# The result stage of an attention and gated feed-forward kernel: fifteen block products of 2x3x3 blocks in place of seven of 2x2x2

## The chip, the cores and the metric

The kernel runs on one core of a Trainium2 chip. The metric is device time in microseconds, from one launch to its end. Three runs of the kernel before took 972.55, 970.60 and 970.07 us, a median of 970.6 us. One profiled execution is described here: its own time was 970.28 us, and the span that its trace covers is 967.9 us, so 2.4 us lie outside the trace.

## The reference, cut to what matters

Banded causal attention (8 batches, 8 heads, 576 positions, head size 64, window 128, with a bias per head), and then a gated feed-forward network over its 4608 tokens:

```python
attn_out = _attn_ref(q, k, v)                     # softmax over a window of 128, times v
x = attn_out.transpose(0, 2, 1, 3).reshape(4608, 512)
gate = 1.0 / (1.0 + np.exp(-(x @ w_gate)))        # w_gate, w_val: 512 x 1536
val = x @ w_val
return (gate * val) @ w_out                       # w_out: 1536 x 512
```

All inputs and outputs are float32, and the kernel's matrix products have float32 accuracy: every operand is split into a rounded part ("hi") and the rest ("lo"), and one product of two operands is three matmuls (hi*hi, lo*hi, hi*lo).

## The kernel before, in words

The work is in three stages. In the first (to about 283 us of the span) the attention of 32 units of two heads runs, and beside it the gate and value projections of the first four feature blocks for the first 2560 tokens (`gates1`, matmuls on L583). In the second (`gates2`, matmuls on L668, 283.65 to 706.72 us) the other projections run. In the third (`results`, matmuls on L794, from 704.00 us) the hidden values, which the stages before left in DRAM (`hs`), are multiplied by `w_out`, and the output is written.

The second and third stages don't multiply blocks one by one. `gates2` takes a round of tokens, cuts it in two halves and the features in two, and forms seven products of sums of blocks where a plain 2x2x2 block product has eight (the products are numbered 0 to 6, made in the order 0, 3, 4, 1, 5, 2, 6). The widths of the halves stand in `HALVES`, one number a round: 512, 384, 384, 512, 512. `results` of before does the same with the hidden values: five rounds of the same widths; the feed-forward dimension is cut in two quadrants of 768 and the tokens in two halves. For each of the seven products it goes through three thirds of 256 features (`e`): it forms the sum of quadrants that the product needs (`add`, L762, in place), splits it into hi and lo (`parts`: a cast by `copy` on L233 or L234, a subtraction by `minus` on L243) and makes two groups of six matmuls (`six`), one for each half `i` of a 256-wide output block. A product ends in two PSUM banks. `keep` (ScalarE, L805) and `total` (VectorE, L810) take the sums out of the banks, and `store` writes them to the output.

The sums of weight blocks are made once, in `combine`: `keepw` first decodes `w_out` (it comes as 64-bit words), writes it to DRAM (`wod`), and `combine` reads it back, makes four sums of 256 columns and splits seven blocks into hi and lo, six times. The tiles `wos` then stay in SBUF for all five rounds.

The order of the work is not written by hand. Each step is added to a graph (`g.add`) with its engine, a cost, what it reads and writes and a wish for its time; `rank` and `order` then lay all steps on the engines' queues by these costs. A step may have several ways: a cast goes to ScalarE or VectorE, a sum that reads no PSUM to VectorE or GpSimd. Each engine works its queue strictly in that order, SyncE (which issues all DMAs) too. The tiles that hold hi and lo of a product (`cxA` with three places, `cxB` with three, `cxC` with one) are used in rotation, so a cast waits until the matmuls that read its place are done.

Of the kernel before, what the change touches and what calls it, by code (L numbers as in the profile page):

```python
# [28 lines left out]
HALVES = (512, 384, 384, 512, 512)  # L29
# [3 lines left out]
HC = NFC // 6  # L33
NRING, NRING1, NHC = 6, 4, 7
# [25 lines left out]
SEEDS = ()  # L60

# [148 lines left out]

@with_exitstack
def attention_gated_ffn(ctx: ExitStack, tc: tile.TileContext, qd, kd, vd, wg, wv, wo, out):
# [24 lines left out]
    def move(out, src, reads, writes, want, kb):  # L237
        g.add("SP", 0.6, lambda: nc.sync.dma_start(out(), src()), reads, writes, want, size=kb / 330.0,
              store=writes[0][0] in ("hs", "xs", "wod", "out"))
# [40 lines left out]
    hs = [[dram.tile([NFC // 2, P, HALVES[b // 2]], F32, name=f"hs{k}_{b}") for b in range(2 * NT2)] for k in range(2)]  # L280
    wod = [dram.tile([P, DM], F32, name=f"wod{f}") for f in range(NFC)]
# [29 lines left out]
    hr = lambda: T(moe, "hr", [P, 2, NFC // 2, N2], F32, tag="wA")  # L311
    hw = lambda: T(moe, "hw", [P, NFC // 2, N2], F32, tag="xW")
# [3 lines left out]
    wot = lambda c, part_: T(name=f"wos{c}", **wtag((c + 4) % 6))[:, part_]  # L316
# [6 lines left out]
    def decode(src, bits, kb, keys, want):  # L323
# [3 lines left out]
        if src.dtype == F32:  # L327
# [3 lines left out]
        g.add("ACT", act_cost(DM), lambda: nc.scalar.mul(as32(bits()), as32(wraw(s)[:, :, 1]), 2.0 ** -112), [kr, *keys], [kb], want)  # L331
        g.add("DVE", dve_cost(DM), lambda: nc.vector.tensor_scalar(
            bits(), bits(), 3, None, op0=ALU.logical_shift_left), [], [kb], want, port=True)
        for word, scalar, o0 in ((0, 29, ALU.logical_shift_right), (1, -0x80000000, ALU.bitwise_and)):
            g.add("DVE", dve_cost(DM, two=True), lambda word=word, scalar=scalar, o0=o0: nc.vector.scalar_tensor_tensor(  # L335
                bits(), wraw(s)[:, :, word], scalar, bits(), op0=o0, op1=ALU.bitwise_or), [kr], [kb], want, port=True)

    def parts(hi, lo, val, n, reads, k0, k1, want):
        copy(hi, val, n, reads, [k0], want)
        minus(lo, val, lambda: as32(hi()), n, [*reads, k0], [k1], want)  # L340
# [398 lines left out]
    hq0 = lambda: T(moe, "hq0", [P, NFC // 2, N2], F32, tag="xr")  # L739
    hquad = lambda h, k: hr()[:, k] if h else hw() if k else hq0()  # L740

    def hcombo(s, part_):
        return combo(ORDER[s], part_)

    def results(t):
        F, N, t0 = FIRST + 2, HALVES[t], EDGE[2 * t]
        third = [slice(e * HC, (e + 1) * HC) for e in range(3)]
        hk = {(h, k, e): [("hq", h, k, e)] for h in range(2) for k in range(2) for e in range(3)}
        for h, k in ((0, 0), (1, 0), (1, 1), (0, 1)):
            for e in range(3):  # L750
                move(lambda h=h, k=k, e=e: hquad(h, k)[:, third[e], 0:N], lambda h=h, k=k, e=e: hs[k][2 * t + h][third[e]].rearrange("c p t -> p c t"),
                     [("hs", k, 2 * t + h, c) for c in range(e * HC, (e + 1) * HC)], hk[h, k, e], F, HC * P * N / 256)
        slots = {(k, e): (3 * n + e) % NHC for n, k in enumerate(ORDER) for e in range(3)}
        m = HC * N

        def split(k, e, val, reads):
            s = slots[k, e]
            parts(lambda: hcombo(s, 0)[:, :, 0:N], lambda: hcombo(s, 1)[:, :, 0:N], val, m, reads, ("hc", s, 0), ("hc", s, 1), F)

        def add(o, a, b, op, reads, writes):  # L760
            way = ("POOL", 0.1 + m * 0.00223, True, lambda: nc.gpsimd.tensor_tensor(o(), a(), b(), op=op))
            g.add("DVE", dve_cost(m, two=True), lambda: nc.vector.tensor_tensor(o(), a(), b(), op=op), reads, writes, F,  # L762
                  port=True, ways=[way])

        bx, bz, by = [], [], []
        some = {}
        bk = lambda b: (lambda: mm[b][:, 0:N])

        halved = lambda k, i: t == NT2 - 1 and k == 6 and i == 1

        def product(k, banks_, start):
            for e in range(3):
                v = lambda a, b, e=e: (lambda: hquad(a, b)[:, third[e], 0:N])
                q = lambda a, b: hk[a, b, e]
                if k == 3:
                    add(v(1, 0), v(1, 0), v(1, 1), ALU.add, q(1, 1), q(1, 0))
                elif k == 4:
                    add(v(1, 0), v(1, 0), v(0, 0), ALU.subtract, q(0, 0), q(1, 0))
                elif k == 5:
                    add(v(0, 1), v(0, 1), v(1, 0), ALU.subtract, q(1, 0), q(0, 1))  # L780
                    add(v(1, 0), v(1, 1), v(1, 0), ALU.subtract, q(1, 1), q(1, 0))
                a, b = {0: (0, 0), 3: (1, 0), 4: (1, 0), 1: (0, 1), 5: (1, 0), 2: (0, 1), 6: (1, 1)}[k]
                split(k, e, v(a, b), q(a, b))
                s = slots[k, e]
                for i in range(2):
                    if len(banks_) == i:
                        banks_.append(bank())

                    last = halved(k, i) and e == 2
                    for a, b in ((0, N // 2), (N // 2, N)) if last else ((0, N),):  # L790
                        def six(i=i, e=e, s=s, a=a, b=b):
                            for c in range(HC):
                                for j, (xp, wp) in enumerate(((0, 0), (0, 1), (1, 0))):
                                    nc.tensor.matmul(mm[banks_[i]][:, a:b], wot(e * HC + c, wp)[:, k, i * P:(i + 1) * P], hcombo(s, xp)[:, c, a:b],  # L794
                                                     start=(start and e == c == j == 0), stop=(e == 2 and c == HC - 1 and j == 2),
                                                     skip_group_check=True)
                        wa = 0 if k < 1 else 1
                        g.add("PE", 3 * HC * ((b - a) / 2400 + 0.0133), six,
                              [("hc", s, 0), ("hc", s, 1)] + [("wo", e * HC + c, p, wa) for c in range(HC) for p in range(2)] + [("mm", banks_[i])] * (a > 0),
                              [("mm", banks_[i], 1) if a else ("mm", banks_[i])], 1.0e6)  # L800

        def keep(name, banks_, i, a=0, e=N):
            s = some[name, i] = some[name, i] if a else scratch()
            b = banks_[i]
            g.add("ACT", act_cost(e - a, psum=True), lambda: nc.scalar.mul(ring2(s)[:, a:e], mm[b][:, a:e], 0.5),  # L805
                  [("mm", b, 1) if a else ("mm", b)], [("rg", s, a) if a else ("rg", s)], F)

        def total(name, banks_, i):
            s, b = some[name, i], banks_[i]
            g.add("DVE", dve_cost(N, psum=True), lambda: nc.vector.scalar_tensor_tensor(  # L810
                ring2(s)[:, 0:N], bk(b)(), 0.5, ring2(s)[:, 0:N], op0=ALU.mult, op1=ALU.add), [("mm", b)], [("rg", s)], F)

        def store(name, i, h, d, a=0, e=N):
            s = some[name, i]
            r = (d * 2 + i) * P
            c0 = t0 + h * N
            move(lambda: out[r:r + P, c0 + a:c0 + e], lambda: ring2(s)[:, a:e], [("rg", s, a) if a else ("rg", s)], [("out", r, c0 + a)], F, (e - a) / 2)

        two = range(2)
        product(0, bx, True)  # L820
        for i in two:
            keep("a1", bx, i)
        product(3, bz, True)
        for i in two:
            keep("p5", bz, i)
        product(4, bx, False)
        for i in two:
            keep("u2", bx, i)
        product(1, by, True)
        for i in two:  # L830
            total("a1", by, i)
            store("a1", i, 0, 0)
        product(5, bx, False)
        for i in two:
            total("p5", bx, i)
            store("p5", i, 1, 1)
        product(2, bz, False)
        for i in two:
            total("u2", bz, i)
            store("u2", i, 0, 1)  # L840
# [126 lines left out]
    for t in range(NT2):  # L967
        results(t)
# [54 lines left out]
```

## Time and profile before

| | |
|---|---|
| median of three runs | 970.6 us (970.07 to 972.55) |
| the profiled execution's own time | 970.28 us |
| its span | 967.9 us |
| TensorE busy (PE) | 959.4 us, 99% of the span |
| VectorE busy (DVE) | 803.7 us, 83% |
| ScalarE busy (ACT) | 502.4 us, 52% |
| GpSimd busy (POOL) | 175.3 us, 18% |
| result stage on TensorE | 704.00 to 964.23 us |

PE are matmuls, PEld the weight loads, which run beside them. A matmul's record reaches from its start to the end of its way through the array and overlaps the next ones, so what a row of matmuls costs is read from the distance between starts, not from the mean duration. The same holds, to a smaller degree, for VectorE's records. The chain of waits names, for each stretch of time, the work that the end of the program waited for.

### The profile page before, as it was taken

The numbers are of one execution on the slowest core, as the hardware profiler recorded it, in microseconds if no ns is written. First come the engines' busy times: TensorE is split into PE (matmuls) and PEld (weight loads), VectorE is DVE, ScalarE is ACT, GpSimd is POOL, SyncE is SP. The second block draws the span as 40 slices with busy tenths as digits, with TensorE's granted clock in tenths as the row PEclk, the third lists the DMA queues.
The fourth block names the chain that finished last, engine by engine and source line by source line (L and its number), as shares of the span: only waits on it lengthen the run. The fifth ranks groups of instructions, "written<-read, shape, count | busy, mean of one in ns | idle before, by whom it ended". The sixth has DMA issues, their size and how long they took to land.

```text
span 967.9 us, 18446 instructions
## 1 busy us (share of the span) xinstructions
PE 959.4 (99%) x6562; PEld 818.0 (85%) x6562; DVE 803.7 (83%) x1807; ACT 502.4 (52%) x1268; POOL 175.3 (18%) x333
## 2 busy tenths in 40 slices
PE   9999999999999999999999999999999999999998
PEld 7777877877788889999988888888888999988887
DVE  7998888999699975475979948897999889898882
ACT  6998978797645543344634434553563233332320
POOL 6555656666301100000000100000000000000000
PEclk9999999999999999999999999999999999999999
DMA  8877767875365313145566512548346263637101
GB/s 305 270 263 267 245 233 256 281 250 189 118 210 175 120 55 128 58 136 169 169 193 204 186 65 75 162 148 280 108 147 190 93 180 101 227 99 238 44 22 65
DMA packets 83610, 162.67 MB, mean 168 GB/s; under 512 B 9408, under 2 KB 35008, under 8 KB 83520
## 3 DMA queue, kind: packets, MB, share of 16 engines
q1 hardware_dynamic: 83520, 161.51, 50.6%
q8 instruction: 51, 0.84, 0.4%
q14 instruction: 39, 0.32, 0.1%
HBM read 111.15 MB, written 50.33 MB: 167 GB/s over the span
## 4 chain that ended last, share of the span: by engine, by line
PE 92%; DVE 4%; ACT 2%; issue 1%; POOL 1%; ACTq 0%; POOLq 0%; DVEq 0%
PE mm L668 44%; PE mm L794 27%; PE mm L583 10%; PE mm L416 5%; PE mm L464 3%; PE mm L525 3%; ACT pb L435 1%; DVE pb L432 1%; PE mm L501 1%; DVE mm L424 1%; DVE pb L458 1%; POOL pt L475 1%; DVE work L335 0%; PE mm L298 0%; DVE x L243 0%
## 5 line engine op out<-in xcount | busy, mean ns | idle before, releaser
L668 PE MATMUL mm<-cxA,w2s 128*128 128x512 f32 (+1 forms) x684 | 161.5, 372 | 0.0
L668 PE MATMUL mm<-cxB,w2s 128*128 128x512 f32 (+1 forms) x684 | 161.4, 372 | 0.0
L233 ACT COPY ring<-mm 128x512 f32<-128x512 f32 (+1 forms) x142 | 78.3, 552 | 130.3 <-PE mm L668 109.3
L668 PEld LDWEIGHTS mm<-cxA,w2s 128*128 128x128 f32 x684 | 125.8, 188 | 18.3
L668 PEld LDWEIGHTS mm<-cxB,w2s 128*128 128x128 f32 x684 | 125.8, 188 | 18.2
L583 PE MATMUL mm<-x,w 128*128 128x512 f32 x480 | 135.0, 411 | 0.0
L435 ACT ACTIVATE pb<-pb,st 128x128 f32<-128x128 f32 x288 | 113.1, 397 | 19.7 <-DVE st L432 18.9
L475 POOL TENSOR_SCALAR_AFFINE_SELECT pt<-both 128x384 f32<-128x384 f32 x192 | 106.5, 579 | 70.5 <-ACT both L233 57.1
L794 PE MATMUL mm<-cxA,wos 128*128 128x512 f32 (+1 forms) x540 | 113.5, 367 | 0.0
L794 PE MATMUL mm<-cxB,wos 128*128 128x512 f32 (+1 forms) x540 | 113.3, 367 | 0.0
L794 PEld LDWEIGHTS mm<-cxA,wos 128*128 128x128 f32 x540 | 98.4, 188 | 12.7
L794 PEld LDWEIGHTS mm<-cxB,wos 128*128 128x128 f32 x540 | 98.4, 188 | 12.6
L583 PEld LDWEIGHTS mm<-x,w 128*128 128x128 f32 x480 | 84.9, 189 | 17.7 <-issue 3.1
L242 POOL TENSOR_TENSOR work<-work 128x256 f32<-128x256 f32 x23 | 20.9, 910 | 420.3 <-DVE work L335 221.3
L679 ACT ACTIVATE sg<-mm 128x512 f32<-128x512 f32 (+1 forms) x96 | 54.1, 564 | 72.9 <-DVE mm L675 42.5
L675 DVE TENSOR_TENSOR mm<-mm,ring 128x512 f32<-128x512 f32 (+1 forms) x96 | 62.2, 649 | 27.4 <-PE mm L668 27.3
L335 DVE SCALAR_TENSOR_TENSOR work<-work 128x512 int32<-128x512 int32 x104 | 69.7, 688 | 0.8
L416 PE MATMUL mm<-kr,qr 64*64 64x192 f32 (+2 forms) x1280 | 67.6, 322 | 1.5 <-DVE st L432 1.3
L432 DVE CUSTOM_DVE_ANT_0 pb<-mm,relm 128x128 f32<-128x128 f32 x288 | 68.6, 278 | 0.0
L424 DVE COPY_PREDICATED mm<-swap,mm 128x256 f32<-128x256 int32 x144 | 55.2, 420 | 12.0 <-PE mm L416 11.9
L416 PEld LDWEIGHTS mm<-kr,qr 64*64 64x64 f32 x1280 | 43.5, 133 | 22.7 <-issue 12.2
L805 ACT ACTIVATE ring<-mm 128x512 f32<-128x512 f32 (+2 forms) x41 | 22.3, 547 | 72.1 <-PE mm L794 72.1
(111 smaller groups left out, 1554.1 us busy)
## 6 DMA issues: line engine op xcount, KB each, us to landing
hs<-ring SPq DMA_DIRECT2D x72, 256.0 KB, 2.4
kr<-in_k_dram SPq DMA_DIRECT2D x31, 576.0 KB, 5.2
work<-in_moe_w_gate_dram SPq DMA_DIRECT2D x20, 512.0 KB, 4.2
work<-in_moe_w_val_dram SPq DMA_DIRECT2D x20, 512.0 KB, 4.5
qr<-in_q_dram SPq DMA_DIRECT2D x31, 320.0 KB, 5.9
vr<-in_v_dram SPq DMA_DIRECT2D x32, 288.0 KB, 4.2
xs<-xt SPq DMA_DIRECT2D x32, 288.0 KB, 4.0
hr<-hs SPq DMA_DIRECT2D x18, 512.0 KB, 4.5
```

What stands on the lines that cost most here:

```text
L233: g.add("ACT", act_cost(n, psum), lambda: nc.scalar.copy(out(), src()), reads, writes, want, release=release, ways=[("DVE", dve_cost(n, ps ...
L335: g.add("DVE", dve_cost(DM, two=True), lambda word=word, scalar=scalar, o0=o0: nc.vector.scalar_tensor_tensor(bits(), wraw(s)[:, :, word], ...
L416: nc.tensor.matmul(sp[j // 2][col, j % 2, c0:c0 + n], qraw(u)[row, i // 2, col], kraw(u)[row, k1:k1 + n], start=True, stop=True)
L424: g.add("DVE", dve_cost(4 * D, psum=True), lambda b=b: nc.vector.copy_predicated(fold[b][:, :, 1:3], swaps, fold[b][:, :, 3::-3]), [], [(" ...
L432: g.add("DVE", 0.21, lambda: nc.vector.tensor_tensor_reduce(pb()[:, e], sp[j // 2][:, j % 2, D:D + P], relm[u.p][:, w], op0=ALU.add, op1=A ...
L435: g.add("ACT", 0.39, lambda: nc.scalar.activation(pb()[:, e], pb()[:, e], AF.Exp, bias=st()[:, e:e + 1], scale=-1.0, accum_out=st()[:, 3 + ...
L475: nc.gpsimd.affine_select(pt(u)[:, f0:f0 + 2 * n - 1:2, :], both(), [[0, n], step], cmp, 0.0, base=0, channel_multiplier=mult)
L583: nc.tensor.matmul(mm[s][:, 0:n], w1(kind, wi)[:, i, c * P:(c + 1) * P], x1(x)[:, c, 0:n], start=(k == 0 and c == 0), stop=(k == 2 and c = ...
L668: nc.tensor.matmul(mm[b][:, 0:N], w2t(i, wp)[:, wk, c * P:(c + 1) * P], combo(k, xp)[:, c, 0:N], start=(start and c == 0 and j == 0), stop ...
L675: g.add("DVE", dve_cost(N, psum=True), lambda: nc.vector.tensor_tensor(o(), bk(b)(), a(), op=ALU.add), [("mm", b), *reads] if okeys else r ...
L679: g.add("ACT", act_cost(N, psum=True), lambda: nc.scalar.activation(sg[h](), bk(b)(), AF.Tanh, scale=0.5), [("mm", b)], [("sg", h)], F)
L794: nc.tensor.matmul(mm[banks_[i]][:, a:b], wot(e * HC + c, wp)[:, k, i * P:(i + 1) * P], hcombo(s, xp)[:, c, a:b], start=(start and e == c ...
```

## The change

The result stage becomes a product of 2 by 3 blocks of `w_out` (256 output columns by 512 features) with 3 by 3 blocks of hidden values (512 features by 512 tokens). A plain product of these blocks has 18 block products; the change makes it with 15 products of sums of blocks. A round is now 1536 tokens, and there are three rounds. Each product runs over 512 features in two halves `h`, and for each half there are a split into hi and lo and two groups of six matmuls, all 512 columns wide. The table `RESULTS` says what is added to what: `wadd` and `wform` make the 15 weight blocks, `x` makes the 15 sums of hidden blocks (13 additions a round, in place, in nine groups of buffers) and says where each product stands between them, `out` says into which PSUM banks (`b`) a product goes, which of them it adds to, and which sums of banks and SBUF buffers (`s`) give the six output blocks (`o`). In a round `out` has 11 sums, each for two halves of a block; 10 of the 11 read a PSUM bank.

`nodes` replaces `keepw` and makes the weight sums from the decoded `w_out`, four times (11 sums of 256 columns and 15 stores to DRAM, `w3d`). `loadw` reads a product's weights back in the first round and splits them (a multiplication on ScalarE and one instruction on VectorE); nine of the 15 stay in SBUF, and six (`STREAM`) are written to DRAM as hi and lo (`w3s`) and read again in each later round, `RECENT` = 3 products ahead. The hi and lo of a half product have five places (`combos`) that go round. Hidden values lie in DRAM in blocks of 512 tokens now, and the second and third round of `gates2` are 256 and 512 wide in place of 384 and 384. All the other code is unchanged but for names.

```diff
-HALVES = (512, 384, 384, 512, 512)
+HALVES = (512, 256, 512, 512, 512)
-HC = NFC // 6
-NRING, NRING1, NHC = 6, 4, 7
+NRING, NRING1 = 6, 4
+NP = 15
+RECENT = 3
+STREAM = (2, 4, 7, 9, 12, 14)
+ROUNDS = (0, 1, 2)
+RESULTS = dict(
+    wadd="6=1-0 7=3-4 8=0+3 9=2+8 10=0+2 11=1+3 12=5+9 14=1+4 13=5+14 15=4+5 16=2+13",
...
-    hs = [[dram.tile([NFC // 2, P, HALVES[b // 2]], F32, name=f"hs{k}_{b}") for b in range(2 * NT2)] for k in range(2)]
-    wod = [dram.tile([P, DM], F32, name=f"wod{f}") for f in range(NFC)]
+    hs = [[dram.tile([KC, P, NB], F32, name=f"hs{k}_{t}") for t in range(NT // NB)] for k in range(3)]
+    w3d = [dram.tile([P, KC, 2 * P], F32, name=f"wd{p}") for p in range(NP)]
+    w3s = [dram.tile([P, KC, 4 * P], F32, name=f"ws{p}") for p in range(NP)]
...
+    def nodes(j):
...
+        for token in RESULTS["wadd"].split():
+            d, x, op, y = term(token)
+            d, x, y = (raw3(int(v)) if int(v) < 6 else int(v) for v in (d, x, y))
+            sums(lambda d=d: piece(d), lambda x=x: piece(x), op, lambda y=y: piece(y), 2 * P, pk(x) + pk(y), pk(d), W)
...
+    combos, banked, rest = Pool((54, 58, 62, 42, 46)), Pool(range(8)), Pool((*range(103, 109), 109, 110, 94))
...
+    def loadw(p, r):
...
+            if r:
+                move(lambda a=a, n=n: at(a, n).rearrange("p (j f) -> p j f", j=n), lambda i=i, n=n: w3s[p][:, i:i + n],
+                     [("w3s", p, j) for j in range(i, i + n)], K(a, n), F, 256 * n)
+                continue
+            move(lambda blk=blk: as32(blk(1)), lambda i=i, n=n: w3d[p][:, i:i + n], [("w3d", p, j) for j in range(i, i + n)], K(a, n), F, 128 * n)
+            m, scale = n * 2 * P, 0.5 if RESULTS["wform"].split()[p][0] == "+" else -0.5
+            g.add("ACT", act_cost(m), lambda blk=blk: nc.scalar.mul(blk(0), as32(blk(1)), scale), [], K(a, n), F)
+            g.add("DVE", dve_cost(m, two=True), lambda blk=blk: nc.vector.scalar_tensor_tensor(
+                blk(1), as32(blk(1)), scale, as32(blk(0)), op0=ALU.mult, op1=ALU.subtract), [], K(a, n), F, port=True)
...
+            for h in range(2):
+                spot = lambda r_: groups[r_] + 2 * h
+                for d, x, op, y in adds:
+                    d, x, y = (spot(int(v)) for v in (d, x, y))
+                    sums(lambda d=d: at(d, 2), lambda x=x: at(x, 2), op, lambda y=y: at(y, 2), 2 * NB, K(x, 2) + K(y, 2), K(d, 2), F)
+                c, o = combos.take(), spot(r)
+                split(c, o)
                 for i in range(2):
+                    def six(h=h, c=c, i=i, b=banks_[i]):
+                        for j in range(2):
+                            for k, (xp, wp) in enumerate(((0, 0), (0, 1), (1, 0))):
...
+                    g.add("PE", 6 * (NB / 2400 + 0.0133), six, K(c, 4) + K(w[2 * h]) + K(w[2 * h + 1]), [("mm", banks_[i])], 1.0e6)
+                combos.give(c)
```

VectorE's queue where the gates end and the result stage begins. Before, a row names the line, the operation, the tile written and the tiles read (`mm` are PSUM banks, `hr`, `hq` and `hw` the hidden values, `cxA` to `cxC` the split sums, `wos` the weights, `ring` and `sg` outputs and gates); it lies near the end of the last gate block:

```order
L243 TENSOR_TENSOR cxA<-hq_6707,cxA 128x1024
L243 TENSOR_TENSOR wos_7059<-work,wos_7059 128x256
L243 TENSOR_TENSOR work<-work 128x256
L243 TENSOR_TENSOR wos_7059<-work,wos_7059 128x1536
L675 TENSOR_TENSOR ring<-mm_145,ring 128x512
L243 TENSOR_TENSOR cxB<-hr,cxB 128x1024 x3
L243 TENSOR_TENSOR wos_7104<-work,wos_7104 128x256
L762 TENSOR_TENSOR hr<-hr,hq_6707 128x1024
L243 TENSOR_TENSOR wos_7104<-work,wos_7104 128x1536
L243 TENSOR_TENSOR cxC<-hr,cxC 128x1024
```

In the changed kernel the same place holds the additions (line 801, `xr`, `work` and `ha` are now the nine groups), the splits (line 277), the gate stage's own sums (lines 712 and 720) and a weight split (line 861); its last row is the sixth split of the first round:

```order
L801 TENSOR_TENSOR xr<-work,xr 128x1024
L720 SCALAR_TENSOR_TENSOR ring<-sg_784,mm_169 128x512
L861 SCALAR_TENSOR_TENSOR w2s_6630<-w2s_6630 128x3x256
L720 SCALAR_TENSOR_TENSOR ring<-sg_985,ring 128x512
L277 TENSOR_TENSOR cxA<-work,cxA 128x1024
L712 TENSOR_TENSOR ring<-mm_170,ring 128x512
L277 TENSOR_TENSOR cxB<-work,cxB 128x1024
L801 TENSOR_TENSOR work<-xr,work 128x1024 x2
L801 TENSOR_TENSOR xr<-xr,ha 128x1024
L277 TENSOR_TENSOR cxB<-work,cxB 128x1024
L801 TENSOR_TENSOR xr<-xr,ha 128x1024
L277 TENSOR_TENSOR cxA<-work,cxA 128x1024
```

The weight sums and splits that make `wos` have left this place; in front of the early products there are more additions than before, and the splits of the 15 weight blocks are spread over the whole first round.

VectorE's queue at the start of a later round. Before (the last round but one), an addition and a split take turns:

```order
L762 TENSOR_TENSOR hr<-hr 128x1024
L243 TENSOR_TENSOR cxA<-hq_6707,cxA 128x1024 x2
L762 TENSOR_TENSOR hr<-hr 128x1024
L243 TENSOR_TENSOR cxA<-hq_6707,cxA 128x1024
L762 TENSOR_TENSOR hr<-hr 128x1024
L243 TENSOR_TENSOR cxB<-hr,cxB 128x1024
L810 SCALAR_TENSOR_TENSOR ring<-mm_146,ring 128x384
L762 TENSOR_TENSOR hr<-hr,hq_6707 128x1024
L243 TENSOR_TENSOR cxB<-hr,cxB 128x1024 x2
```

In the changed kernel the second round begins so (from its fourth split to its eighth):

```order
L277 TENSOR_TENSOR cxB<-work,cxB 128x1024
L801 TENSOR_TENSOR work<-xr,work 128x1024
L801 TENSOR_TENSOR xr<-work,xr 128x1024
L801 TENSOR_TENSOR xr<-xr,ha 128x1024
L277 TENSOR_TENSOR cxB<-work,cxB 128x1024
L801 TENSOR_TENSOR work<-xr,work 128x1024
L801 TENSOR_TENSOR work<-work,xr 128x1024
L801 TENSOR_TENSOR xr<-xr,ha 128x1024
L277 TENSOR_TENSOR cxA<-work,cxA 128x1024 x2
L801 TENSOR_TENSOR work<-work,xr 128x1024
L801 TENSOR_TENSOR ha<-ha,xr 128x1024 x2
L277 TENSOR_TENSOR cxA<-work,cxA 128x1024
```

Nine additions stand between five splits here, where before there were four between six.

## Rows read from the trace of the kernel before

**Rows 1.** The page's busy times: engine, us, share of the span, instructions.

```profile
PE 959.4 (99%) x6562; PEld 818.0 (85%) x6562; DVE 803.7 (83%) x1807; ACT 502.4 (52%) x1268; POOL 175.3 (18%) x333
```

**Rows 2.** Chain of waits, in order of time: start us, us, what.

```profile
298.64 405.36 PE mm L668 x1944
704.00 1.36 PE mm L794 x6
...
706.72 257.51 PE mm L794 x1260
```

**Rows 3.** Busy time by stretch: the five result rounds (the second row holds two).

```profile
core 0: us, PE busy (x) PEld busy (x) DVE busy (x) ACT busy (x) POOL busy (x), PEclk, DMA share, GB/s
706.70:763.40 56.70, 56.70 (x254) 47.13 (x253) 53.37 (x59) 22.26 (x27) 0.00 (x0) 1.00 0.54 172
763.40:850.60 87.20, 87.20 (x503) 87.06 (x502) 76.05 (x92) 30.00 (x42) 0.00 (x0) 1.00 0.49 152
850.60:907.60 57.00, 57.00 (x253) 47.18 (x252) 50.42 (x50) 18.00 (x22) 0.00 (x0) 1.00 0.46 150
907.60:964.40 56.80, 56.62 (x256) 46.96 (x254) 35.14 (x37) 10.50 (x15) 0.00 (x0) 1.00 0.09 35
```

**Rows 4.** Timeline of TensorE: start us, us, what; 384 wide, then 512 wide.

```profile
399.62 1.20 PE L668 MATMUL mm<-cxB,w2s 128*128 128x384 f32 x6
400.66 1.20 PE L668 MATMUL mm<-cxA,w 128*128 128x384 f32 x6
...
944.95 8.32 PE L794 MATMUL mm<-cxA,wos 128*128 128x512 f32 x36
953.11 8.32 PE L794 MATMUL mm<-cxB,wos 128*128 128x512 f32 x36
```

**Rows 5.** Timeline of the end, all engines; the 18 are 6 of 512 and 12 of 256 columns.

```profile
961.04 2.97 PEld L794 LDWEIGHTS mm<-cxC,wos 128*128 128x128 f32 x18
961.27 2.95 PE L794 MATMUL mm<-cxC,wos 128*128 128x512 f32 x18
...
964.26 0.66 ACT L805 ACTIVATE ring<-mm 128x256 f32<-128x256 f32 x2 [0.83 <-PE mm L794]
```

**Rows 6.** Groups by shape, 704 to 968 us: busy us, mean ns, idle before, releaser.

```profile
L794 PEld LDWEIGHTS mm<-cxB,wos 128*128 128x128 f32 x540 | 98.4, 188 | 12.6
...
L233 ACT CAST cxB<-hr 128x1024 fp32r<-128x1024 f32 x13 | 13.7, 1053 | 27.7 <-PE mm L794 24.4 <-DVE hr L762 3.3
...
L810 DVE SCALAR_TENSOR_TENSOR ring<-mm,ring 128x512 f32<-128x512 f32 x18 | 12.3, 687 | 8.4 <-PE mm L794 8.4
...
L794 PE MATMUL mm<-cxC,wos 128*128 128x256 f32 x12 | 1.6, 282 | 0.0
```

**Rows 7.** Timeline of VectorE in stretches where it did not wait.

```profile
701.64 0.41 DVE L243 TENSOR_TENSOR wos<-work,wos 128x256 fp32r<-128x256 f32 x1
701.98 0.42 DVE L243 TENSOR_TENSOR work<-work 128x256 f32<-128x256 f32 x1
702.31 1.75 DVE L243 TENSOR_TENSOR wos<-work,wos 128x1536 fp32r<-128x1536 f32 x1
...
889.74 0.68 DVE L810 SCALAR_TENSOR_TENSOR ring<-mm,ring 128x512 f32<-128x512 f32 x1
890.34 1.22 DVE L762 TENSOR_TENSOR hr<-hr 128x1024 f32<-128x1024 f32 x1
891.48 0.68 DVE L810 SCALAR_TENSOR_TENSOR ring<-mm,ring 128x512 f32<-128x512 f32 x1
892.08 1.22 DVE L243 TENSOR_TENSOR cxA<-hq,cxA 128x1024 fp32r<-128x1024 f32 x1
893.21 1.22 DVE L762 TENSOR_TENSOR hr<-hr 128x1024 f32<-128x1024 f32 x1
```

**Rows 8.** Busy time by stretch (columns as in rows 3): two with much DMA.

```profile
0.00:24.20 24.20, 22.40 (x254) 18.48 (x255) 18.36 (x96) 15.81 (x61) 16.07 (x33) 1.00 0.85 305
...
653.40:677.60 24.20, 24.20 (x109) 20.04 (x108) 18.76 (x29) 8.74 (x15) 1.75 (x2) 1.00 0.83 280
```

More of the change, by code (lines that the diff above doesn't have):

```diff
@@ L208, in act_cost, with term, __init__, take @@
     return (0.05 if psum else 0.1) + n * 0.00084
+def term(token):
+    dst, val = token.split("=")
+    op = next(c for c in val if c in "+-_")
+    a, b = val.split(op)
+    return dst, a, op, b
+class Pool:
+    def __init__(self, free):
+        self.free = list(free)
+        self.low = len(self.free)
+    def take(self):
+        x = self.free.pop(0)
+        self.low = min(self.low, len(self.free))
+        return x
+    def give(self, x):
+        self.free.append(x)
 @with_exitstack
@@ L737, in mix @@
         yield 6
[L739 to L784, printed above, removed]
-                for i in range(2):
[L786 to L840, printed above, removed]
-        product(6, bx, False)
-        for i in two:
-            for a, b in ((0, N // 2), (N // 2, N)) if halved(6, i) else ((0, N),):
-                keep("x", bx, i, a, b)
-                store("x", i, 1, 0, a, b)
@@ new lines, in loadh @@
+    def loadh(r, s):
+        k, t = r // 3, 3 * s + r % 3
+        for h in range(2):
+            move(lambda h=h: at(groups[r] + 2 * h, 2).rearrange("p (c t) -> p c t", c=2),
+                 lambda h=h: hs[k][t][2 * h:2 * h + 2].rearrange("c p t -> p c t"),
+                 [("hs", KC * k + 2 * h + c, t) for c in range(2)], K(groups[r] + 2 * h, 2), FIRST + 2, 512)
+    want3 = []
+    for token in RESULTS["x"].split():
+        for r in ([token.split(":")[1]] if token[0] == "p" else term(token)[1::2]):
+            if ("h", int(r)) not in want3:
+                want3.append(("h", int(r)))
+        if token[0] == "p":
+            want3.append(("w", int(token[1:].split(":")[0])))
@@ L847, in attention_gated_ffn, with ahead @@
+    def ahead(n):
+        while upcoming and upcoming[0][0] <= n and (upcoming[0][1] and upcoming[0][2] not in STREAM or len(homes.free) >= KC):
+            _, q, i = upcoming.pop(0)
+            loadw(i, q)
     units = [Unit(n) for n in range(B * NPAIR)]
@@ L861, in attention_gated_ffn @@
         load(units[n])
-    at = 0
+    pos = 0
     for u in units:
@@ L935, in drain @@
             pass
+    for j in range(KC):
+        nodes(j)
     for t in range(EARLY):
```

228 lines of the change are left out of this document (190 added, 38 removed).

## The prediction

> **What bounds the kernel now.** I read the busy times first, then the chain of waits, then the busy times round by round, then the distances between starts on TensorE and VectorE. TensorE is busy for 99% of the span [rows 1], and the chain lies on its matmuls through the whole second and third stage [rows 2]: 405.36 us of gate products from 298.64 us, then 1.36 + 257.51 = 258.87 us of result products, to 706.72 + 257.51 = 964.23 us. The reader is to see that there are no other pieces between them. So a stage costs its number of matmuls times the distance of their starts, as long as nobody is late. Who could be late is VectorE: in the result rounds its records fill 53.37 of 56.7 us, 76.05 of 87.2, 50.42 of 57.0 [rows 3], while ScalarE has over half its time free and GpSimd does nothing. The granted clock is 1.00 there, the 2.4 GHz level.
>
> **Matmuls removed.** Starts of 36 matmuls of 512 columns lie 953.11 - 944.95 = 8.16 us apart, 0.2267 us each; six of 384 columns 1.04 us, 0.1733 each [rows 4]. At the end, 6 of 512 and 12 of 256 columns start between 961.27 and about 963.94 (the piece ends 0.28 us after its last start): 11 distances in 963.94 - 961.27 - 6 x 0.2267 = 1.31 us, so 0.120 us each [rows 5, 6]. Before, a round has 7 products x 3 thirds x 2 halves x 6 = 252 matmuls: 3 rounds x 252 x 0.2267 + 2 x 252 x 0.1733 = 258.7 us, which agrees with the chain's 258.87. After, 15 products x 2 halves x 2 x 6 = 360 a round, 1080 in all, x 0.2267 = 244.8 us. **-14.0 us.**
>
> **Gates.** Two rounds of 336 matmuls of 384 columns, 116.5 us, become 336 x 0.120 + 336 x 0.2267 = 116.5 us: **0**. What speaks against it is the weight load: its record is 0.188 us long in the mean [rows 6], longer than 0.120. But in [rows 5] 18 loads end 2.97 us after the first began, and 12 of them at the short distance. The Trainium skill, TensorE: Matmul & The Clock Gate, section The mechanism, says that a weight load overlaps matmuls in flight only when its row group differs; all matmuls here use all 128 rows, so by that rule load and matmul would add. The row contradicts it, and the measurement decides; it stays as a rival below, worked out from the rows.
>
> **VectorE in the result stage.** This term decides how much of the 14 us stays. Records of VectorE overlap, so I take distances between starts [rows 7]: 1.135 us for a sum or split of 1024 elements (892.08 to 893.21, 890.34 to 891.48), 0.60 for one of 512 with a bank, 0.33 for 256. A weight split of 1024 elements is not in the trace; the nearest rows are the split of 1024 (1.135) and that of 1536 (703.98 - 702.31 = 1.67, or 1.11 for 1024): between 1.11 and 1.22 (the record), taken 1.135. Weight splits of 768 and 512 elements go between these distances: 0.87 and 0.60.
>
> A half product of two groups of six takes TensorE 12 x 0.2267 = 2.72 us, and a round of 30 takes 81.6. VectorE's queue in the second round of the changed order has 30 splits, 25 additions, 20 sums with banks and 2 without: 55 x 1.135 + 22 x 0.60 = 75.6 us. So in the later rounds it just keeps up. In the first round come 15 weight splits (15 x 1.135 = 17 us), some of them ahead of its start. There the queue is the slower one.
>
> I follow the two queues with T, the end of the last gate matmul (706.72 us in the span, as the gates cost the same). On TensorE one group of six of the first half product stands before T, so half n (from 1) starts at T + (n - 1.5) x 2.72: the sixth at 12.2. On VectorE the queue is still held by the gates at its sum of a bank that is filled 11 groups of six before T (T - 15.0); from there to the end of the sixth split stand 19.0 us of rows (first and last: that bank sum, and the last row of the first changed block shown), and one addition with its split right behind, where the split waits for the cast on ScalarE between them (1.05 us [rows 6], 1.2 with the signals). With 0.3 for the first signal: T + 5.5. VectorE leads by 6.7 us.
>
> From the sixth split to the 38th (eighth of the second round, the last row shown) VectorE has 32 splits and 30 additions (62 x 1.135 = 70.4), 26 sums of 512 (15.6) and weight splits for 10.6: 96.6 us. TensorE has 32 x 2.72 = 87.0. The lead of 6.7 shrinks by 9.6, so TensorE loses **+2.9 us**. From there to the 90th VectorE has 130.2 us of rows against 52 x 2.72 = 141.4: the lead comes back, and nothing more is lost.
>
> **What that leaves out.** VectorE also waits: for casts, for banks, for DMA. Below: none, 0. Above: a wait of 0.47 us before each of the 10 pairs of bank sums of the first round, as before L810 now (8.4 us for 18 [rows 6]), 4.7 us, and a DMA share below. I take **+2**, since the order was made for TensorE running ahead of what it will get, so most banks are full when VectorE comes. DMA: by the changed order about 32 MB move from T - 15 to T + 92 (first hidden blocks, weights, six weights written, outputs, next blocks), 303 GB/s, while the trace has a stretch at 305 GB/s with share 0.85 and one at 280 with 0.83 [rows 8]. It fits, barely. The weight loads of later rounds (12 MB) lie in 194 GB/s. Weight preparation before T trades 12 decodes for the same 12, and 24 sums for 44 (16 on GpSimd, which is idle) in a stage where VectorE has room; 0. The tail: the last output is 512 wide where now it is 256, so half of ScalarE's 0.66 us for two [rows 5] comes on top: **+0.3** on the 3.7 us from the last matmul to the end of the span.
>
> **Sum.** 970.28 - 14.0 + 0 + 2.9 + 2 + 0.3 = 961.5 us for an execution like the profiled one, which lies 0.3 below the median of the runs, inside their spread; I forecast **961.5 us**. What is called the same is within 0.3%, 2.9 us.
>
> **Rivals.**
> 1. *No loss at all.* Weight splits go early enough, and TensorE never waits: 970.28 - 14.0 + 0.3 = 956.6. Against it: the first round's 9.6 us. Chance 0.15, from 956 to 958.
> 2. *DMA fills the first round.* 32.4 MB at 280 GB/s (the second stretch of [rows 8]) take 116 us where 107 are there: 9 more, of which what VectorE and TensorE have ahead covers little; 961.5 + 7 = 968.5. For it: the share of 0.83 at 280. Against it: 305 in the first stretch. Chance 0.14.
> 3. *VectorE's waits for banks decide.* VectorE's queue is in order, and 10 pairs of bank sums a round, 30 in all, stand between splits. If each pair waits w for TensorE's product, the split behind it is late, and then the matmuls behind that split, which fill the next bank. The queue ends its 90th split at T + 5.5 + 226.8 + 30 w, and the last half product ends 2.72 later: T + 235.0 + 30 w, against T + 257.5 before. From w = 0.75 on it is slower than before; at w = 1.0: 706.72 + 265.0 + 3.9 + 2.4 = 978.0 us. For it: one row waits 0.47 in the mean now. Against it: those waits come with an engine that is ahead; behind schedule it finds banks full. Chance 0.11.
> 4. *VectorE is slower than its distances.* If the records' lengths (1.22, 0.69) and not the distances are what a row costs, the same sums give the sixth split at T + 7.2 and 247.1 us to the 90th, T + 257.0 for the last matmul, 970.0. Against it: [rows 7]. Chance 0.06.
> 5. *Weight loads set 256-column matmuls.* 336 x (0.188 - 0.120) = 23 us: 984. Chance 0.01.
>
> The forecast's own case, 958 to 966, has 0.53. So faster: 0.53 + 0.15 + 0.11 (most of 2) = 0.79; same: 0.09 (rest of 2, most of 4); slower: 0.12 (3, 5). The range 956 to 971 leaves out 3, 5, and the far end of 2.
>
> **What would show it.** In the changed profile: 1080 result matmuls 0.2267 us apart where TensorE doesn't wait; waits of TensorE for VectorE's splits in the first round and up to about 87 us after its start, 3 to 5 us in all, and next to none later; VectorE without idle time in that stretch; 128x256 gate matmuls 0.120 us apart. Wrong would be: waits of TensorE in the later rounds, VectorE idle for TensorE before bank sums (rival 3), waits for loads from `wd` or `ws` (rival 2), or a result stage of 245 us without a gap (rival 1).

## The result and the profile after

The changed kernel takes **960.67 us** (median, 960.35 to 961.16); the kernel before takes 970.87 us in the same comparison. The ratio is 0.9893, with a 95% interval of 0.9876 to 0.991: faster, by 10.2 us, clear of the 0.3% (2.9 us) within which the prediction calls two times the same. The forecast was 961.5 us. The profiled execution took 961.16 us with a span of 959.5 us.

The busy times of the changed kernel, to be laid beside [rows 1]:

```profile
PE 947.6 (99%) x6376; PEld 778.1 (81%) x6376; DVE 825.5 (86%) x1823; ACT 538.7 (56%) x1306; POOL 190.1 (20%) x348
```

TensorE has less to do and still fills the span, and VectorE has more. The chain of waits, which answers [rows 2], shows what is between TensorE's pieces now (start us, us, what):

```profile
286.17 183.25 PE mm L705 x966
...
481.59 224.75 PE mm L705 x990
706.35 1.36 PE mm L946 x6
707.71 1.36 PE mm L705 x6
709.07 1.37 PE mm L946 x6
...
788.99 2.35 DVE cxA L277 x2
803.89 1.23 DVE cxA L277
805.16 35.44 PE mm L946 x154
841.32 114.54 PE mm L946 x504
```

The last gate matmul ends at T = 709.07, the last result matmul at 841.32 + 114.54 = 955.86: 246.79 us, where it was 257.51. Without a wait 1074 matmuls would take 243.5, so TensorE loses 3.3 us, and all of it before 841.32: after that the chain is one piece of TensorE. Where it loses, the timeline of TensorE shows (start us, us, what, idle before and releaser); the two rows of the gate stage ahead of them are 256 columns wide:

```profile
363.74 0.88 PE L705 MATMUL mm<-cxA,w2s 128*128 128x256 f32 x6
364.46 0.88 PE L705 MATMUL mm<-cxB,w2s 128*128 128x256 f32 x6
...
786.27 4.56 PE L946 MATMUL mm<-cxB,w2s 128*128 128x512 f32 x18 [0.45 <-DVE mm L801]
...
798.82 5.60 PE L946 MATMUL mm<-cxB,w2s 128*128 128x512 f32 x24
804.26 0.61 PE L946 MATMUL mm<-cxA,w2s 128*128 128x512 f32 x2
805.16 8.24 PE L946 MATMUL mm<-cxA,w2s 128*128 128x512 f32 x34 [0.28 <-DVE cxA L277]
813.24 5.60 PE L946 MATMUL mm<-cxB,w2s 128*128 128x512 f32 x24
...
832.28 8.32 PE L946 MATMUL mm<-cxA,w2s 128*128 128x512 f32 x36
841.32 3.01 PE L946 MATMUL mm<-cxB,w2s 128*128 128x512 f32 x12 [0.72 <-issue]
...
923.04 1.52 PE L946 MATMUL mm<-cxB,w2s 128*128 128x512 f32 x6
```

Idle time is printed only from 0.2 us on, so read the distances. From 798.82 to 804.26 are 24 matmuls, 0.2267 us each: no loss. From 804.26 to 813.24 are 36, which need 8.16 and take 8.98: 0.82 lost. From 832.28 to 841.32 another 0.88. Six such places (in order of time 0.19, 0.41, 0.61, 0.31, 0.82, 0.88) make 3.2 us. The busy times of the three rounds, beside [rows 3]:

```profile
core 0: us, PE busy (x) PEld busy (x) DVE busy (x) ACT busy (x) POOL busy (x), PEclk, DMA share, GB/s
709.00:790.60 81.60, 81.01 (x355) 66.02 (x354) 81.60 (x90) 44.13 (x57) 0.00 (x0) 1.00 0.66 229
790.60:874.10 83.50, 82.50 (x362) 67.37 (x362) 83.50 (x86) 39.50 (x46) 0.00 (x0) 1.00 0.72 250
874.10:955.90 81.80, 81.74 (x361) 67.37 (x359) 70.52 (x73) 32.15 (x37) 0.00 (x0) 1.00 0.41 143
```

VectorE has no idle time for two rounds. Full does not mean late, though: what counts is its **lead**, the start of a half product's first matmul minus the end of the record of the split that it reads. In the timeline of VectorE, the first of two splits in one record ends at 803.89 + 1.22 = 805.11, and the matmul that reads it starts at 805.16. The other rows are a split and two bank sums (sums that read a PSUM bank) ahead of the wait that ends at 841.32, and the same sum one round later:

```profile
803.89 2.35 DVE L277 TENSOR_TENSOR cxA<-work,cxA 128x1024 fp32r<-128x1024 f32 x2
...
838.26 1.21 DVE L277 TENSOR_TENSOR cxB<-ha,cxB 128x1024 fp32r<-128x1024 f32 x1
...
840.54 1.28 DVE L801 TENSOR_TENSOR mm<-sg,mm 128x512 f32<-128x512 f32 x2
...
921.88 0.70 DVE L801 TENSOR_TENSOR mm<-sg,mm 128x512 f32<-128x512 f32 x1
```

So TensorE waits for two kinds of rows. The 0.82 us around 805.16 are late splits. At 841.32 the split was in time: it was done at 838.26 + 1.21 = 839.47, 1.85 us ahead. What ends just before the matmul, at 841.22, is the first of the two bank sums. By the table `RESULTS` (`8+b4 b5=s3+b4 9+b4`) that sum must read bank b4 before the next product adds to it, and the product before fills the bank only one group of six, 1.36 us, before TensorE comes back to it. So this sum can't be made ahead, however far VectorE leads with its splits: in the third round, where nothing waits, it ends at 922.58, 0.46 us before its matmul (923.04). The places of 0.41 us (a matmul at 778.75, a sum that ends at 778.61) and of 0.61 (786.27) follow bank sums too. About 1.9 of the 3.2 us are lost behind bank sums that stand late in VectorE's full queue, and 0.8 behind splits; the 0.19 and 0.31 are not told apart here.

VectorE's own waits, from the list of waits between 690 and 960 us (who, for whom: us in total, times, longest), are small in the result stage (the line left out is for a bank of the gates):

```profile
...
DVE w2s L861 <- ACT w2s L860: 0.8, 1, 0.8
DVE cxA L277 <- ACT cxA L267: 0.5, 2, 0.3
DVE cxB L277 <- ACT cxB L267: 0.5, 2, 0.2
DVE cxB L268 <- PE mm L946: 0.4, 1, 0.4
```

The lead at five half products, worked out this way from the timelines of four kernels (us; the largest is that behind the first four, which fill empty buffers):

| half product | 6 | 20 | 36 | 50 | 79 | largest |
|---|---|---|---|---|---|---|
| changed kernel | 7.1 | 0.4 | -0.8 | 1.2 | 3.5 | 8.9 |
| e1, no weight splits on VectorE | 4.2 | 1.9 | 7.5 | 4.0 | 3.5 | 8.9 |
| e8, four split buffers | 4.8 | 1.2 | -0.2 | 1.1 | 1.8 | 6.2 |
| e10, splits in the gate stage | 7.2 | 3.7 | 7.5 | 4.0 | 3.5 | 9.0 |

(The first two matmuls of a half product read only what ScalarE casts, so a lead down to -0.45, two distances, makes no wait.)

### The profile page after: what moved, and what is told of

Read it like the earlier page. It is cut to its first block, busy times and chain, and to the rows that moved or that the text cites. A ratio compares the mean times of both kernels' runs of the same rounds, so it can differ in the third digit from the quotient of the medians.

```text
span 959.5 us, 18276 instructions
## 1 busy us (share of the span) xinstructions
PE 947.6 (99%) x6376; PEld 778.1 (81%) x6376; DVE 825.5 (86%) x1823; ACT 538.7 (56%) x1306; POOL 190.1 (20%) x348
## 4 chain that ended last, share of the span: by engine, by line
PE 82%; DVE 12%; issue 2%; POOL 2%; ACT 1%; DMA 1%; SPq 0%; POOLq 0%; DVEq 0%; ACTq 0%
PE mm L705 43%; PE mm L946 16%; PE mm L620 10%; PE mm L453 5%; PE mm L501 3%; PE mm L562 3%; DVE cxA L277 2%; DVE cxB L277 1%; PE mm L538 1%; DVE work L801 1%; DVE w2s L861 1%; DVE ha L801 1%; DVE xr L801 1%; DVE pb L469 1%; DVE ring L801 1%
## 5 line engine op out<-in xcount | busy, mean ns | idle before, releaser
L267 ACT COPY ring<-mm 128x512 f32<-128x512 f32 (+1 forms) x161 | 89.2, 556 | 148.3 <-PE mm L705 109.3
L705 PEld LDWEIGHTS mm<-cxA,w2s 128*128 128x128 f32 x684 | 122.3, 188 | 22.9 <-DVE cxA L277 0.4
L705 PEld LDWEIGHTS mm<-cxB,w2s 128*128 128x128 f32 x684 | 122.3, 188 | 22.6 <-DVE cxB L277 0.2
L946 PE MATMUL mm<-cxA,w2s 128*128 128x512 f32 x576 | 134.8, 390 | 0.4 <-DVE cxA L277 0.3
L946 PEld LDWEIGHTS mm<-cxA,w2s 128*128 128x128 f32 x576 | 107.9, 188 | 23.9 <-DVE cxA L277 1.1
L946 PE MATMUL mm<-cxB,w2s 128*128 128x512 f32 x432 | 102.0, 390 | 1.2 <-issue 0.7
L946 PEld LDWEIGHTS mm<-cxB,w2s 128*128 128x128 f32 x432 | 80.8, 188 | 19.3 <-DVE mm L801 1.2
L472 ACT ACTIVATION_READ_ACCUMULATOR pb<-pb,st 128x1 f32 x288 | 55.4, 192 | 0.0
```

Source lines behind the costliest of these rows:

```text
L267: g.add("ACT", act_cost(n, psum), lambda: nc.scalar.copy(out(), src()), reads, writes, want, release=release, ways=[("DVE", dve_cost(n, ps ...
L472: g.add("ACT", 0.39, lambda: nc.scalar.activation(pb()[:, e], pb()[:, e], AF.Exp, bias=st()[:, e:e + 1], scale=-1.0, accum_out=st()[:, 3 + ...
L705: nc.tensor.matmul(mm[b][:, 0:N], w2t(i, wp)[:, wk, c * P:(c + 1) * P], combo(k, xp)[:, c, 0:N], start=(start and c == 0 and j == 0), stop ...
L946: nc.tensor.matmul(mm[b], at(w[2 * h + j], 1, True)[:, f:f + P], at(c + 2 * xp + j, 1, True), start=(start and h == j == k == 0), stop=(h ...
```

## Experiments

The theory after the result: 14 us of matmuls saved, less 3.3 us that TensorE waits for VectorE, whose queue is too full in the first round because of the weight splits, so that splits and bank sums come late. Rivals: the first round is full of transfers; waits for signals and banks; the other widths of the gate rounds. The kernel before, run again beside the experiments, took 971.31 us (e1, e2, e3, e5), 971.17 (e4, e6, e7, e8) and 971.0 (e9, e10, e11) in place of 970.87, so differences below half a microsecond are not read.

**e1: VectorE without the weight splits.** The kernel leaves out the low parts of the result weights: a plain multiplication on ScalarE stands in their place.

```diff
-            g.add("DVE", dve_cost(m, two=True), lambda blk=blk: nc.vector.scalar_tensor_tensor(
-                blk(1), as32(blk(1)), scale, as32(blk(0)), op0=ALU.mult, op1=ALU.subtract), [], K(a, n), F, port=True)
+            g.add("ACT", act_cost(m), lambda blk=blk: nc.scalar.mul(blk(1), as32(blk(1)), scale), [], K(a, n), F)
```

> The 24 weight splits of VectorE (about 17 us of rows, all for the first round) are replaced by 24 plain multiplications on ScalarE; the low parts of the result weights are thereby wrong in value. The planner answers by putting 7 casts and a copy on VectorE (about 5 us). Theory (VectorE's full queue in the first round costs TensorE about 3.2 us): the loss goes, last gate matmul to last result matmul 243.8 to 245 us instead of 246.96, time 957.3 to 958.8. Rival (DMA fills the first round) and rival (waits for signals and banks): nothing changes, 960.7 +- 0.6.

Measured: 956.69 us (956.61 to 956.9). The end of its chain of waits is one piece:

```profile
707.81 243.53 PE mm L945 x1074
```

All 3.3 us are gone, a little more than expected in the time. With this the -14.0 us of the matmuls is measured too: 257.51 to 243.5. Both rivals fall: the transfers and the bank sums are as many as before.

**e2 and e3: VectorE with more work, early and late.** The same subtraction issued twice, in the first round (e2: `q == 0 and 3 <= p <= 5`) or in the third (e3: `q == 2 and 3 <= p <= 6`):

```diff
                 split(c, o)
+                if q == 0 and 3 <= p <= 5:
+                    minus(lambda c=c: at(c + 2, 2, True), lambda o=o: at(o, 2), lambda c=c: as32(at(c, 2, True)), 2 * NB, [*K(o, 2), *K(c, 2)], K(c + 2, 2), F, pool=False)
```

> Six subtractions of a split (1024 elements) are issued a second time in products 3 to 5 of the FIRST round: 6 x 1.135 = 6.8 us more on VectorE. Theory: TensorE already waits for VectorE there, so all of it comes through: 967.5 (966 to 968.5). Rival DMA, or waits for signals: VectorE has air, 960.7 to 962.

> Eight such second subtractions in products 3 to 6 of the THIRD round; three casts leave VectorE at the same time: 8 x 1.135 - 3 x 0.6 = 7.3 us more on VectorE. Theory: from the 38th split on VectorE gains 0.215 us on TensorE with every half product, 6.4 us by the 68th and 8 us by the 75th, so next to nothing comes through: 960.7 to 962. Rival (VectorE's full row length counts, no air anywhere): 7 us come through, 967 to 968.

Measured: e2 968.84 (967.01 to 970.04), e3 963.98 (963.09 to 966.09), both above their ranges. Early work comes through in full, +8.2 for 6.8. Late work comes through in part, +3.3 for 7.3, which is more than the theory allowed. Two causes are in the profiles. First, the air: by the table VectorE's lead never passes about 9 us and falls to 3.5 at half product 79 of a third round with five buffers. There TensorE waits in e3, and again for the bank sum, which in the changed kernel has 0.46 us to spare; the split that half product 79 reads was done 1.8 us earlier. That 7.3 us do not fit into this is shown by the wait, but not worked out. Second, the clock. VectorE's bank sum in e3, TensorE's timeline, and its busy times before and after that wait:

```profile
925.47 1.30 DVE L801 TENSOR_TENSOR mm<-sg,mm 128x512 f32<-128x512 f32 x2
```

```profile
926.28 4.56 PE L948 MATMUL mm<-cxB,w2s 128*128 128x512 f32 x12 [2.90 <-issue]
930.64 1.58 PE L948 MATMUL mm<-cxA,w2s 128*128 128x512 f32 x6
```

```profile
915.00:923.38 8.38, 8.38 (x37) 6.59 (x36) 8.38 (x10) 3.26 (x5) 0.00 (x0) 1.00 0.58 188
926.28:930.64 4.36, 4.36 (x13) 3.42 (x13) 4.36 (x5) 0.52 (x2) 0.00 (x0) 0.62 0.00 0
```

The granted clock is 0.62 in the 4.36 us after the wait (between the levels of 1.2 and 2.4 GHz), and 12 matmuls take 4.36 in place of 2.72: the wait of 2.9 costs 1.6 more. In e2 the same follows a wait of 3.13 us. The executions of both kernels with a mean clock of 1.000 are the shortest, 967.0 (+6.3) and 963.1 to 964.0 (+2.4 to +3.3). So the clock explains why e2 came out above 6.8, and the two longest executions of e3 (965.7 and 966.1), but not its median, which is one of clock 1.000.

**e5: twice the stores of the streamed weights.**

```diff
+                move(lambda i=i, n=n: w3x[p][:, i:i + n], lambda a=a, n=n: at(a, n).rearrange("p (j f) -> p j f", j=n),
+                     K(a, n), [("w3s", p + NP, j) for j in range(i, i + n)], F, 256 * n)
```

> The six streamed weights are written twice (the second time to DRAM tiles nobody reads): 6.3 MB more in the first round, 17 us of all the queues at the 366 GB/s seen there. Theory (VectorE decides): 960.7 to 962. Rival (DMA fills the first round): hidden blocks and weights come later by 10 us or more, 968 to 978, with waits of VectorE for loads.

Measured: 962.49 us (961.36 to 964.22), +1.8, half a microsecond above the range. The 17 us of transfers are nearly all hidden. In its chain of waits a few are not:

```profile
729.94 7.28 DMA wx<-w2s
...
813.39 7.94 DMA cxC<-hs
```

So the transfers do not set the first round, but they have little room left.

**e8: four split buffers in place of five.** `combos = Pool((54, 58, 62, 42))`, without 46.

> Four buffers for the split hidden blocks in place of five. Theory (the lead of VectorE over TensorE is capped by these buffers: it never passes 8.9 us in the changed kernel, and falls by up to 7 us where additions stand together, at half products 18 to 20, 48 to 50, 78 to 80): the cap falls by one half product, 2.7 us, to 6.2, and 1.5 to 2.5 us more are lost in the first two rounds: 962.2 to 963.2. Rival (the lead is set by something else, banks or the hidden blocks' loads): 960.7.

Measured: 963.73 us (962.69 to 964.25), +3.1, as expected in kind and 0.5 above the range. The cap on the lead fell from 8.9 to 6.2, one half product of 2.7 us. Who waits for the buffers is ScalarE, whose cast is their first writer; its list of waits between 700 and 950 us says

```profile
ACT cxA L267 <- PE mm L946: 50.9, 35, 4.4
ACT cxB L267 <- PE mm L946: 21.6, 13, 4.4
```

72.5 us together, where the changed kernel has 15.5 + 26.5 = 42.0. TensorE loses its time at half products 19, 49 and 79 (1.94, 2.03 and 0.68 us), each time behind the bank sum of the half product.

**e4: the old widths of the gate rounds.** `HALVES = (512, 384, 384, 512, 512)`.

> The changed kernel with the old widths of the gate rounds (512, 384, 384, 512, 512) in place of 512, 256, 512, 512, 512. Theory (336 x 0.120 + 336 x 0.2267 = 2 x 336 x 0.1733, so the widths are worth nothing): 960.7, within 0.8; six matmuls of 384 columns 1.04 us. Rival (the widths are part of the 10 us, by weight loads or by the later first stage of the profiled run): 2 us or more to either side.

Measured: 966.21 us (965.2 to 966.98), **+5.5, against the theory**. The result stage is not the place: it takes 246.99 us from T to the last matmul, as in the changed kernel. TensorE waits in the gate stage (by the timeline 2.89 us at 559 to 562 and 1.42 at 481, where the changed kernel waits 1.08), and SyncE issues the load of the next gate weights late. From the timelines of TensorE and SyncE in e4:

```profile
559.28 0.50 PE L705 MATMUL mm<-cxA,w2s 128*128 128x512 f32 x1 [1.03 <-ACT w2s L267]
561.65 4.62 PE L705 MATMUL mm<-cxA,w2s 128*128 128x512 f32 x12 [1.86 <-DVE w2s L277]
```

```profile
539.63 0.38 SPq L272 DMA_DIRECT2D wd<-work  x1
...
542.33 0.43 SPq L272 DMA_DIRECT2D work<-in_moe_w_gate_dram  x1
```

Behind the second wait the granted clock is 0.61 for 4.4 us, as in e3. The tile `work` holds first the result weights' combinations (`nodes`), then the raw gate weights. These can only be loaded when the last combination has been stored (`wd<-work`). In the changed kernel the same two stand earlier, and there is no wait at 555 to 562:

```profile
531.91 1.39 SPq L272 DMA_DIRECT2D wd<-work  x3
...
534.34 0.45 SPq L272 DMA_DIRECT2D work<-in_moe_w_gate_dram  x1
```

**e7: no sums on GpSimd.** `ways = []` in `sums`.

> The 15 sums of the result weights that the planner gave to GpSimd in the gate stage stand on VectorE (15 x 0.33 = 5 us more there). Theory (VectorE's rows of 1024 elements took 1.75 us in place of 1.21 while GpSimd worked, and TensorE waited 1.08 us at 481.6): the wait goes, the rows are 1.21 us again, 959.6 (959.0 to 960.2). Rival (VectorE was late there of itself): the wait stays or grows by part of the 5 us, 960.7 to 962.

Measured: 965.17 us (964.49 to 967.16), **+4.5, against both**. The wait at 481.6 did go, and its cause is as stated. VectorE's timeline in the changed kernel, then GpSimd's, then VectorE's in e7:

```profile
472.94 1.76 DVE L754 TENSOR_TENSOR xr<-xr 128x1024 f32<-128x1024 f32 x1
474.62 1.23 DVE L720 SCALAR_TENSOR_TENSOR ring<-sg,ring 128x512 f32<-128x512 f32 x1
475.77 0.69 DVE L712 TENSOR_TENSOR mm<-mm,ring 128x512 f32<-128x512 f32 x1
...
479.19 1.75 DVE L754 TENSOR_TENSOR xr<-xr 128x1024 f32<-128x1024 f32 x1
```

```profile
466.98 0.74 POOL L802 TENSOR_TENSOR work<-work 128x256 f32<-128x256 f32 x1 [2.28 <-DVE work L371]
469.62 10.23 POOL L802 TENSOR_TENSOR work<-work 128x256 f32<-128x256 f32 x8 [1.90 <-ACT cxA L267]
```

```profile
477.49 1.22 DVE L754 TENSOR_TENSOR xr<-xr 128x1024 f32<-128x1024 f32 x1
...
479.23 1.22 DVE L754 TENSOR_TENSOR xr<-xr 128x1024 f32<-128x1024 f32 x1
```

But with 15 sums more on VectorE the combinations are done later, the load of the gate weights is issued at 540.23, and TensorE waits 1.25, 0.53 and 1.23 us at 554 to 560. These are the signs of e4's handover again; e7 was not run with the load put forward, so that the 15 sums themselves make VectorE late is not excluded.

**e9 and e11: the handover put forward.** `HORIZON = 70.0` in place of 40.0 lets loads stand earlier in the planner; e9 is e4 with it, e11 the changed kernel with it.

> The kernel with the old gate widths (966.2 us; TensorE waits 4.3 us at 559 to 562 us for the weights of the last gate rounds), with the planner's HORIZON raised from 40 to 70: the result weights' combinations start earlier, and the loads of the gate weights, which need the same work tile, stand four stores of hidden blocks earlier in SyncE's queue. Theory (the gate weights are late because the work tile is handed over late: first load issued at 542 us, in the changed kernel at 534): most of the wait goes, 961.5 to 963. Rival (VectorE has too much work there at these widths): 965.5 to 967.

> The changed kernel with HORIZON 70 alone, the control for the two others. The work tile is handed over in time already; theory: 960.7, or 959.6 if the one wait of 1.08 us at 481.6 moves away with GpSimd's sums; rival (HORIZON itself speeds up or slows down the first or the result stage): 2 us or more to either side.

Measured: e9 959.92 us (959.53 to 960.32), e11 959.86 us (959.1 to 960.58). In e9 the load is issued at 524.06 in place of 542.33, and TensorE's gate stage is one piece of its chain of waits:

```profile
285.31 420.05 PE mm L705 x2010
```

So the 5.5 us of e4 were the handover, all of them: 6.3 came back, more than expected, and 0.8 of that is what e11 gains, where the wait at 481.6 is gone as well, as the sums stand elsewhere. (The 0.8 is small beside the spreads of the two, 960.35 to 961.16 and 959.1 to 960.58.) With the handover in time the two sets of widths differ by 0.06 us.

**e6 and e10: a version that keeps VectorE free in the first round.** High and low parts of all fifteen weights are formed in `nodes` and stored, and the first round loads them; e10 is e6 with `HORIZON = 70.0`. The core of it:

```diff
+            g.add("ACT", act_cost(2 * P), lambda o=o, v=v, scale=scale: nc.scalar.mul(round3(o), piece(v), scale), pk(v), pk(o), W)
+            g.add("DVE", dve_cost(2 * P, two=True), lambda o=o, v=v, scale=scale: nc.vector.scalar_tensor_tensor(
+                round3(v), piece(v), scale, piece(o), op0=ALU.mult, op1=ALU.subtract), pk(o), pk(v), W, port=True)
+            move(lambda p=p: w3s[p][:, j, 0:2 * P], lambda o=o: piece(o), pk(o), [("w3s", p, j)], W, 128)
+            move(lambda p=p: w3s[p][:, j, 2 * P:], lambda v=v: piece(v), pk(v), [("w3s", p, j, 1)], W, 128)
```

> The high and low parts of all fifteen weights are formed in the gate stage (60 ScalarE multiplications and 60 VectorE splits of 256 elements, 0.33 us each, 20 us of VectorE there) and stored; the first round only loads them, 7.9 MB more to load and 6.3 MB less to store. Theory (VectorE's 17 us of weight splits in the first round cost TensorE 3.4 us): the loss goes as in e1, 956.7 if the gate stage hides the 20 us, up to 958.5 if it makes a new wait there; last gate to last result matmul 243.5 to 244. Rival DMA: the first round is limited by its transfers, 960 or more.

> The kernel with the weight splits in the gate stage (960.0 us; no wait in the result stage, some in the gate stage) with HORIZON 70. Theory: the waits that this kernel has left in its gate stage (0.8 us, 445 to 484 us) come from decodes and splits crowded into that stretch; started earlier they spread: 957.5 to 959.3, result stage 243.5. Rival: what is left is not in the gate stage, 960.

Measured: e6 959.98 us (959.24 to 960.37), which misses its range, and e10 **958.57 us** (958.07 to 959.2), a ratio to the kernel before of 0.9874 (0.9859 to 0.9888): the fastest of the kernels that compute the whole result. Both have the result stage without a wait (e10's chain of waits):

```profile
710.27 243.45 PE mm L938 x1074
```

What they pay is in the gate stage: TensorE waits 0.24, 0.22 and 0.38 us in e6 and 0.62, 0.21 and 0.83 us in e10, where the 60 splits crowd. So the waits did not spread with the larger `HORIZON`, as was expected, but grew from 0.84 to 1.66 us, and the gate stage of e10 is no shorter than that of e6 (423.96 and 423.82 us from the seventh gate matmul to the last). In the profiled executions the difference stands in the first stage, which ended 0.97 us earlier in e10; why is not shown.

## Why the prediction was right, and where it was not

The time was forecast within 1 us. Its steps did less well than that, and some of the agreement is luck.

- **Matmuls removed, -14.0.** Right: 257.51 to 243.5 us where nothing waits (e1, e6, e10).
- **Gates, 0.** Right for the matmuls: six of 256 columns start 0.72 us apart, 0.120 each, though the loads beside them are 0.188 long in the mean in [rows 6]. By the sentence of the Trainium skill, TensorE: Matmul & The Clock Gate, section The mechanism, on which the prediction drew, load and matmul would have added; this trace contradicts it. The same section also says that a load into the background weight buffer is pulled ahead of matmuls in flight, and the 0.120 fits that.
- **Weight preparation "in a stage where VectorE has room; 0".** This step failed. It counted VectorE's time and not the tile `work`, through which result weights and gate weights pass one after the other, nor what GpSimd's sums do to VectorE. In the profiled run it cost the wait of 1.08 us at 481.59; with the old widths it cost 4 to 6 us (e4, e9), and with VectorE in GpSimd's place 4.5 (e7). The new widths came with it and happened to be in time.
- **VectorE's lead, TensorE loses 2.9.** That VectorE's queue with the weight splits is the slower one, and that TensorE pays for it, was right, and e1 shows it. The lead at the sixth split was 7.1 us (worked out: 6.7; the 0.3 and 0.15 us for signals in that sum rest on no row, and here 0.05 us lie between the end of a split and the matmul that waited for it, 805.11 and 805.16), and 2.3 us were lost by the 38th. But the sum sets splits alone against matmuls, and most of the loss came behind bank sums, for which VectorE cannot lead. "The lead comes back, and nothing more is lost" was wrong by 0.9 us, at such a sum, 841.32. The lead was also taken to change evenly, while it falls by 4 to 7 us where additions stand together (half products 18 to 20, 48 to 50, 78 to 80), and it cannot be saved up beyond about 9 us, the five buffers (e8). That is also where e3 lost more than its range allowed.
- **Waits left out, +2.** Not there: VectorE waited 2.2 us in the result stage, and not before its bank sums. The 3.3 us lost stand against 2.9 + 2.
- **Tail, +0.3.** 0: from the last matmul to the end of the span are 959.5 - 955.86 = 3.64 us, where it was 3.7.
- **Outside the sum.** By the chains of waits the first stage was 1.2 us longer in the profiled execution (286.17 less 1.36 for six gate matmuls that now stand ahead of that piece, against 283.65). Its granted clock was 0.78 from 40 to 45 us, after waits of 0.87 and 0.97 us, and 26 matmuls took 3.64 us that take 2.08 in e1, where the same waits stand and the clock stays at 1.00. The time around the span was 0.7 us less. For the profiled execution the loss of the result stage (1.6 less than 2.9 + 2), the tail (0.3) and the time around the span (0.7) stand against about 1.2 us in the first stage and 1.1 in the gate stage: they nearly cancel, and that is luck.

Of the rivals, *no loss at all* (956.6) is what e1 measures when its condition is made true, 956.69, though e1 keeps the wait of the gate stage, so that an agreement within 0.1 us is chance. *DMA* falls with e1 and e5, and of the 32 MB worked out for T - 15 to T + 92 the trace has 27 (253 GB/s from 694 to 801 us, at a share of 0.73); *VectorE's waits for banks* with the list of waits, *records as cost* with the lead of 7.1, *weight loads* with the 0.120.

Not settled: why the clock drops at 40 us in the profiled execution of the changed kernel and not in that of e1, after the same waits.

## What to carry to other kernels

When two engines are nearly balanced, follow the lead of the feeding engine through the whole program, with its cap (the buffers between them) and its dips (rows that stand together); a busy share of 100% says nothing about lateness. Follow every kind of row that the fed engine waits for: a sum that has to read a bank between two products that fill it has a lead of its own, and a small one. When work moves into a stage "with room", ask not only which engine has time but which buffer it holds and who is waiting to have it. An edit that is worth nothing by itself can carry microseconds through the schedule, so test it with that schedule's slack restored.

## What the hardware showed that was not expected

- **A wait of TensorE can cost more than its length.** After waits of 2.90 (e3) and 3.13 us (e2) the granted clock was 0.62 and 0.64 over the next 4.4 and 4.5 us, 1.6 us lost on top. After two waits with one matmul between, 1.03 and 1.86 us, it was 0.61 (e4); after single waits of 1.78 and 1.87 us in e8 it stayed at 1.00.
- **GpSimd slows VectorE.** While GpSimd ran its sums, several of VectorE's rows with both inputs in SBUF took 1.75 in place of 1.22 us (1024 elements) and 1.23 in place of 0.69 (512), and GpSimd's own 10.23 / 8 = 1.28 in place of 0.74 (0.74 to 1.77 each); the row with a bank as input stayed at 0.69. The Trainium skill, SBUF — State Buffer, section Who interferes with whom, says that a VectorE instruction with two SBUF inputs contends with a GpSimd one that reads SBUF; the trace agrees.
